# A long convolution beside local attention on one core: one manual order for the projections and the kernel generation, and a convolution in channel halves

## The chip, the core and the metric

The kernel runs on one core of a Trainium2 chip. A core has five engines with their own instruction streams: TensorE (PE in the profile, with its weight loads shown as PEld), VectorE (DVE), ScalarE (ACT), GpSimd (POOL) and SyncE (SP). Data moves between DRAM and the on-chip memory through 16 DMA engines; a transfer is started by an instruction on SP, ACT or POOL. Matmul results land in PSUM, a small memory that ACT and DVE read.

The metric is device time of one execution in microseconds (us). Lower is better. The runs of one kernel mostly agree within about 1%. Each run is marked fast or slow by its time and by the granted TensorE clock (the share of full speed at which the chip let TensorE run, 1.00 being full speed).

## The reference, cut to what matters

Two independent heads are computed and their outputs are put side by side.

```python
# head A: a state-space convolution over L = 2048 steps, D = 1024 channels, N = 128 states
P = exp(dt*A * l)                       # complex, for every step l
K = einsum("dn,dnl,dn->dl", C, P, dt*B).real          # one filter of 2048 taps per channel
y = irfft(rfft(pad(u)) * rfft(pad(K)))[:L] + u * Dskip

# head B: dilated local attention, 32 heads of 32, window 8, dilation 2
q, k, v = split(x @ wqkv)               # x is 2048 x 1024, wqkv 1024 x 3072
o = softmax(q . k[pos - 2*w], w = 0..7) @ v[pos - 2*w]
out_b = o @ wo
```

All inputs and outputs are bf16. Both kernels do the convolution as a two-step FFT with constant matrices: "step 1" multiplies u and K by a 128-wide matrix and stores the results Zu and Zk in DRAM in another order; the "middle" loads them back, transforms them further, multiplies, transforms half the way back and stores Zv (called Vd in the kernel before); "last" reads that and makes the output. Each Z array is 8.4 MB.

## The kernel before

It has three stages: (1) the projections beside the generation of K, with V after Q and K; (2) what is left of K, with step 1 of u; (3) the rest of the convolution beside attention. The parts that matter here are these (cuts are marked with "...").

```python
# V: 4096 matmuls of 128 columns
for half in range(2):
    for kt in range(KT):
        for h in range(4):
            nc.tensor.matmul(pv[32 * h:32 * h + 32, b, half * 4:half * 4 + 4, :], lhsT=xT[:, kt, t0:t0 + 32], rhs=wv[half][:, kt, :, h, :],
                             start=(kt == 0), stop=(kt == KT - 1), tile_position=(0, 32 * h))
...
# K generation: evacuation of a chunk
nc.scalar.copy(out=kraw[:, :, q0:q0 + 32].rearrange("p r (b q) -> p b q r", b=2), in_=pkv)
...
# attention: softmax without a division, by Exp and Ln in turn
nc.scalar.activation(out=pe[:], in_=S[:, :, 0:320], func=ACT.Exp, scale=scale)
...
nc.scalar.activation(out=ln[:], in_=O[:, 1, :], func=ACT.Ln)
nc.scalar.activation(out=ln[:], in_=ln[:], func=ACT.Exp, scale=-1.0)
...
# middle of the convolution: everything out of PSUM by ACT
s3 = sb.tile([128, 3, 512], BF, name="s3", bufs=4)
nc.scalar.copy(out=s3[:], in_=p3[:])
...
nc.vector.tensor_tensor(out=t12[:], in0=s3[:, 0:1, :].to_broadcast([128, 2, 512]), in1=s3[:, 1:3, :], op=ALU.mult)
...
nc.scalar.copy(out=vs[:, h * 512:(h + 1) * 512], in_=pv[:])
...
nc.scalar.dma_start(out=Vd[ri, k], in_=vs[ri * 64:(ri + 1) * 64, :])
...
# the order of the stages
_interleave([ga, gb], [1, 2], stop_on=1)                       # K generation, projections
_interleave([conv_pre(tc, S, A_u[0], "Zu", side="right"), ga], [2, 1], stop_on=0)
...
_interleave([ga, gb], [1, 1])                                  # convolution, attention
```

The softmax here doesn't subtract the row's maximum and nothing guards it: scores larger than these inputs give would overflow.

Of the kernel before, what the change touches and what calls it, by code (L numbers as in the profile page):

```python
# [18 lines left out]
def to_chunks(t):  # L19
    return t.rearrange("p (c g q) -> p g c q", c=4, g=4)  # L20


def natural(t):
    return t.rearrange("p (g c q) -> p g c q", c=4, g=4)


def kgen_params(tc, pp, tmp, A_re,A_im,B_re,B_im,C_re,C_im,log_dt):
    nc=tc.nc; V=nc.vector
    raw={}
    for nm,ap in (("Are",A_re),("Aim",A_im),("Bre",B_re),("Bim",B_im),("Cre",C_re),("Cim",C_im)):  # L30
        t=tmp.tile([128,1024],BF,name="r"+nm)
        nc.sync.dma_start_transpose(out=t[:],in_=ap)
        raw[nm]=t
    ldt=tmp.tile([128,1024],BF,name="ldt")
    nc.sync.dma_start(out=ldt[:],in_=log_dt.unsqueeze(0).to_broadcast([128,1024]))
    dt=tmp.tile([128,1024],BF,name="dt")
    nc.scalar.activation(out=dt[:],in_=ldt[:],func=ACT.Exp)
    a=pp.tile([128,1024],F32,name="p_a"); xs=pp.tile([128,1024],F32,name="p_xs")
    lnW=tmp.tile([128,1024],F32,name="lnW"); Wm=pp.tile([128,1024],BF,name="p_Wm"); phs=pp.tile([128,1024],F32,name="p_phs")
    V.tensor_tensor(out=to_chunks(a[:]),in0=natural(dt[:]),in1=natural(raw["Are"][:]),op=ALU.mult)  # L40
    v=tmp.tile([128,1024],F32,name="v"); ti=tmp.tile([128,1024],I32,name="ti")
    V.tensor_tensor(out=to_chunks(v[:]),in0=natural(dt[:]),in1=natural(raw["Aim"][:]),op=ALU.mult)
    cst=float(65536/TWO_PI)
    V.tensor_scalar(out=ti[:],in0=v[:],scalar1=cst,scalar2=None,op0=ALU.mult)
    V.scalar_tensor_tensor(out=xs[:],in0=v[:],scalar=cst,in1=ti[:],op0=ALU.mult,op1=ALU.subtract)
    lo=ti[:].bitcast(I16).rearrange("p (n two) -> p n two",two=2)[:,:,0]
    V.tensor_tensor(out=xs[:],in0=xs[:],in1=lo,op=ALU.add)
    wre=tmp.tile([128,1024],F32,name="wre"); wim=tmp.tile([128,1024],F32,name="wim"); t1=tmp.tile([128,1024],F32,name="t1"); t2=tmp.tile([128,1024],F32,name="t2")
    V.tensor_tensor(out=wre[:],in0=raw["Cre"][:],in1=raw["Bre"][:],op=ALU.mult)
    V.tensor_tensor(out=t1[:],in0=raw["Cim"][:],in1=raw["Bim"][:],op=ALU.mult)  # L50
    V.tensor_tensor(out=wre[:],in0=wre[:],in1=t1[:],op=ALU.subtract)
    V.tensor_tensor(out=wre[:],in0=wre[:],in1=dt[:],op=ALU.mult)
    V.tensor_tensor(out=wim[:],in0=raw["Cre"][:],in1=raw["Bim"][:],op=ALU.mult)
    V.tensor_tensor(out=t1[:],in0=raw["Cim"][:],in1=raw["Bre"][:],op=ALU.mult)
    V.tensor_tensor(out=wim[:],in0=wim[:],in1=t1[:],op=ALU.add)
    V.tensor_tensor(out=wim[:],in0=wim[:],in1=dt[:],op=ALU.mult)
    V.tensor_tensor(out=t1[:],in0=wre[:],in1=wre[:],op=ALU.mult)
    V.tensor_tensor(out=t2[:],in0=wim[:],in1=wim[:],op=ALU.mult)
    V.tensor_tensor(out=t1[:],in0=t1[:],in1=t2[:],op=ALU.add)
    V.tensor_scalar(out=t1[:],in0=t1[:],scalar1=1e-36,scalar2=None,op0=ALU.add)  # L60
    nc.scalar.activation(out=lnW[:],in_=t1[:],func=ACT.Ln)
    nc.scalar.activation(out=to_chunks(Wm[:]),in_=natural(lnW[:]),func=ACT.Exp,scale=0.5)
    ax=tmp.tile([128,1024],F32,name="ax"); ay=tmp.tile([128,1024],F32,name="ay")
    nc.scalar.activation(out=ax[:],in_=wre[:],func=ACT.Abs)
    nc.scalar.activation(out=ay[:],in_=wim[:],func=ACT.Abs)
    V.tensor_tensor(out=t1[:],in0=ax[:],in1=ay[:],op=ALU.max)
    V.tensor_tensor(out=t2[:],in0=ax[:],in1=ay[:],op=ALU.min)
    V.tensor_scalar(out=t1[:],in0=t1[:],scalar1=1e-30,scalar2=None,op0=ALU.add)
    V.reciprocal(out=t1[:],in_=t1[:])
    V.tensor_tensor(out=t2[:],in0=t2[:],in1=t1[:],op=ALU.mult)  # L70
    at=tmp.tile([128,1024],F32,name="at")
    nc.scalar.activation(out=at[:],in_=t2[:],func=ACT.Arctan)
    V.tensor_tensor(out=t1[:],in0=ay[:],in1=ax[:],op=ALU.is_gt)
    V.tensor_scalar(out=t2[:],in0=at[:],scalar1=-2.0,scalar2=float(np.pi/2),op0=ALU.mult,op1=ALU.add)
    V.tensor_tensor(out=t2[:],in0=t2[:],in1=t1[:],op=ALU.mult)
    V.tensor_tensor(out=at[:],in0=at[:],in1=t2[:],op=ALU.add)
    V.tensor_single_scalar(out=t1[:],in_=wre[:],scalar=0.0,op=ALU.is_lt)
    V.tensor_scalar(out=t2[:],in0=at[:],scalar1=-2.0,scalar2=float(np.pi),op0=ALU.mult,op1=ALU.add)
    V.tensor_tensor(out=t2[:],in0=t2[:],in1=t1[:],op=ALU.mult)
    V.tensor_tensor(out=at[:],in0=at[:],in1=t2[:],op=ALU.add)  # L80
    V.tensor_scalar(out=t1[:],in0=wim[:],scalar1=0.0,scalar2=-2.0*cst,op0=ALU.is_lt,op1=ALU.mult)
    V.tensor_scalar(out=t1[:],in0=t1[:],scalar1=cst,scalar2=None,op0=ALU.add)
    V.tensor_tensor(out=to_chunks(phs[:]),in0=natural(at[:]),in1=natural(t1[:]),op=ALU.mult)
    return a,xs,Wm,phs
# [15 lines left out]
def kgen(ctx, tc, A_re, A_im, B_re, B_im, C_re, C_im, log_dt, Dskip, Kd, pre=None):  # L100


    nc = tc.nc; V = nc.vector
    NCH = 4; CH = 256; Q = 64; DH = CH // 4
    pp = ctx.enter_context(tc.tile_pool(name="k_par", side="left", bufs=1))
    with tc.tile_pool(name="k_tmp", side="left", bufs=1) as tmp:
        a, xs, Wm, phs = kgen_params(tc, pp, tmp, A_re, A_im, B_re, B_im, C_re, C_im, log_dt)
        if pre is not None:
            yield from pre
    yield  # L110
    kr = ctx.enter_context(tc.tile_pool(name="k_raw", side="left", bufs=1))
    kraw = kr.tile([128, NR, 256], BF, name="kraw")
    shs, odds = shift_consts()
    shd = nc.inline_tensor(np.ascontiguousarray(shs.transpose(1, 0, 2)), name="c_sh")
    odd_d = nc.inline_tensor(odds, name="c_odd")
    shsb = kr.tile([128, 2, 128], BF, name="shsb"); odd = kr.tile([128, 2], F32, name="odd")
    nc.sync.dma_start(out=shsb[:], in_=shd.ap())
    nc.sync.dma_start(out=odd[:], in_=odd_d.ap())
    dsk = kr.tile([128, 256], BF, name="dsk")
    V.memset(dsk[:], 0.0)  # L120
    for g in range(4):
        nc.sync.dma_start(out=dsk[32 * g:32 * g + 1, :], in_=Dskip.rearrange("(o g q) -> g o q", o=1, g=4)[g])
    low16 = lambda t: t.bitcast(I16).rearrange("p j (dh dl two) -> p j dh dl two", dl=4, two=2)[:, :, :, :, 0]
    with ExitStack() as c1:
        op = c1.enter_context(tc.tile_pool(name="k_op", side="left", bufs=1))
        ph = c1.enter_context(tc.tile_pool(name="k_ph", side="left", bufs=2))
        ps = c1.enter_context(tc.tile_pool(name="k_ps", side="left", bufs=1, space=PSUM))

        E4 = pp.tile([128, 12, 1024], BF, name="E4")
        for i in range(4):  # L130
            nc.scalar.activation(out=E4[:, i, :], in_=a[:], func=ACT.Exp, scale=float(64 * i))
        for j in range(8):
            nc.scalar.activation(out=E4[:, 4 + j, :], in_=a[:], func=ACT.Exp, scale=float(8 * j))
        blk = lambda t: t.rearrange("p (dh dl) -> p dh dl", dl=4)
        for c in range(NCH):
            cs = slice(c * CH, (c + 1) * CH)
            xc = xs[:, cs]; ac = a[:, cs]; pc = phs[:, cs]; E4c = E4[:, :, cs]
            OL = op.tile([128, 2, DH, 32, 4], BF, name="OL")
            OR = op.tile([128, 2, DH, NR, 4], BF, name="OR")
            TL = op.tile([128, 2, DH, 17, 4], BF, name="TL")  # L140
            ER = op.tile([128, DH, NR, 4], BF, name="ER")
            for j, r in enumerate(RS):
                nc.scalar.activation(out=ER[:, :, j, :], in_=blk(ac), func=ACT.Exp, scale=float(r))
            yield
            for k, n in ((0, 5), (5, 4), (9, 4), (13, 4)):
                PH = ph.tile([128, 2, 5, CH], I32, name="PH")
# [3 lines left out]
                for ri in range(2):  # L150
                    nc.scalar.activation(out=TL[:, ri, :, k:k + n, :].rearrange("p dh j dl -> p j dh dl"), in_=low16(PH[:, ri, 0:n, :]), func=ACT.Sin, scale=SINSC)
# [307 lines left out]
def conv_gen(ctx, tc, S, Kd_in, outa):  # L459
# [3 lines left out]
    with ExitStack() as c2:  # L463
# [39 lines left out]
        for t in range(32 + 2):  # L503
            if t < 32:
                stage_a(t)
# [117 lines left out]
```

## Time and profile before

| | before |
|---|---|
| median of 2 runs | 906.24 us (904.7 to 907.78) |
| span of the profiled run | 907.0 us, mean granted TensorE clock 0.786 |
| busy, share of the span | PE 56%, ACT 62%, DVE 32% |
| DMA | 118.65 MB in 83,431 packets |

No engine is the limit over the whole span, so the profile has to be read by stage. The windows view of the kernel before gives, for each stretch of time, its length, each engine's busy time with its instruction count, the granted TensorE clock, the busy share of the 16 DMA engines, and GB/s:

```profile
core 0: us, PE busy (x) PEld busy (x) DVE busy (x) ACT busy (x) POOL busy (x), PEclk, DMA share, GB/s
0.00:182.00 182.00, 123.69 (x1077) 57.28 (x1088) 117.68 (x177) 117.06 (x140) 0.20 (x4) 0.95 0.44 116
182.00:300.00 118.00, 68.92 (x4127) 63.31 (x4127) 17.83 (x48) 31.92 (x46) 0.00 (x0) 0.93 0.12 40
300.00:450.00 150.00, 43.80 (x1515) 22.73 (x1519) 75.18 (x115) 89.84 (x91) 0.00 (x0) 0.56 0.41 116
450.00:545.00 95.00, 38.16 (x1115) 18.13 (x1129) 8.09 (x14) 54.52 (x61) 0.00 (x0) 0.59 0.75 220
545.00:835.00 290.00, 197.64 (x3955) 88.77 (x3985) 73.12 (x113) 244.83 (x269) 84.45 (x160) 0.81 0.51 148
```

From 182 to 300 us the core does V alone, with ACT busy 32 and DVE 18 of 118 us; from 300 to 450 it finishes K with TensorE at half clock; from 545 to 835 ACT is busy for 245 of 290 us. Two pieces of the chain of waits (start, duration, what) show what V's stretch and the end are made of; the rows between and around are left out:

```profile
239.51 1.97 PE ps L298 x128
241.48 2.03 issue
243.51 1.97 PE ps L298 x128
245.48 1.48 issue
...
870.05 20.35 DMA v<-Vd
```

About two fifths of V's time is not matmul but "issue", time in which the engine waited for nothing that the profile shows (47.4 us beside 69.4 of matmul, first row of the next view). At the end, TensorE waits 20 us for the last step's input. The groups view (line, engine, operation, shapes, count; busy us and mean ns; then idle time before them with its causes) shows V's matmuls and where ACT's time goes:

```profile
L298 PE MATMUL ps<-w,xT 128*32 128x128 bf16 x4096 | 69.4, 230 | 52.7 <-issue 47.4
L486 ACT CAST s<-p 128x1536 bf16<-128x1536 f32 x64 | 91.7, 1433 | 27.6 <-PE p L484 14.8 <-DVE pm L363 12.2 <-PE pv L498 0.6
L382 ACT ACT_TABLE_LOAD x32 | 41.1, 1283 | 10.6 <-issue 10.2
L383 ACT ACT_TABLE_LOAD x31 | 39.8, 1283 | 0.5
L185 ACT CAST kraw<-pk 128x672 bf16<-128x672 f32 x8 | 25.3, 3163 | 42.7 <-PE pk L182 42.7
```

The 63 table loads of attention, from Exp to Ln and back, cost 81 us of ACT.

### The profile page before, as it was taken

How to read it: one execution, taken by the hardware profiler on the slowest of the kernel's cores; microseconds unless marked ns; L12 is line 12 of the kernel's file. 1: busy time of each engine (PE TensorE's matmuls, PEld its weight loads, DVE VectorE, ACT ScalarE, POOL GpSimd, SP SyncE). 2: the span in 40 equal slices, each digit the busy share in tenths (PEclk: the TensorE clock that was granted, in tenths of full speed). 3: DMA queues.
4: the chain of work that ended last, by engine and by line, in shares of the span. 5: the costliest groups of instructions: out<-in, count | busy, mean ns of one | idle time of the engine just before them, and what ended most of it. 6: DMA issues, size and time to landing. Idle time of an engine off the chain costs nothing.

```text
span 907.0 us, 26183 instructions
## 1 busy us (share of the span) xinstructions
PE 506.7 (56%) x11984; PEld 263.9 (29%) x12046; DVE 292.6 (32%) x467; ACT 561.0 (62%) x628; POOL 84.6 (9%) x164
## 2 busy tenths in 40 slices
PE   0395997865555445111205464866785668754823
PEld 0142444365545211111102221332332323322301
DVE  5967841980000071487301110223222332221000
ACT  3558783781111386791308685799979997897323
POOL 0000000000000000000000002533243233300000
PEclk9997998979899666555556568977798779885977
DMA  8922323310111376600597566644584335516484
GB/s 168 197 74 92 124 74 96 102 37 35 37 51 39 124 200 177 181 2 1 125 280 253 186 160 221 201 119 117 170 248 148 104 111 153 165 33 151 107 222 148
DMA packets 83431, 118.65 MB, mean 131 GB/s; under 512 B 29941, under 2 KB 59001, under 8 KB 79737
## 3 DMA queue, kind: packets, MB, share of 16 engines
q1 hardware_dynamic: 56440, 48.80, 20.3%
q10 hardware_dynamic: 19200, 46.15, 16.6%
q0 software_dynamic: 7680, 22.03, 8.4%
q8 instruction: 94, 1.54, 0.7%
q14 instruction: 17, 0.13, 0.0%
HBM read 60.85 MB, written 50.33 MB: 123 GB/s over the span
## 4 chain that ended last, share of the span: by engine, by line
ACT 31%; PE 29%; issue 18%; DMA 7%; DVE 6%; SPq 5%; ACTq 3%; another core or an unknown queue 0%; POOL 0%; DVEq 0%
PE ps L279 11%; PE ps L298 8%; ACT s L486 6%; ACT zsb L427 4%; PE S L390 4%; ACT L383 3%; SPq L259 2%; ACT L382 2%; DMA v<-Vd 2%; ACT kraw L185 2%; ACT ln L382 2%; ACT ln L383 2%; ACT pe L361 2%; PE pz L426 2%; SPq L215 2%
## 5 line engine op out<-in xcount | busy, mean ns | idle before, releaser
L279 PE MATMUL ps<-xT,w 128*128 128x512 bf16 x501 | 117.7, 396 | 48.0 <-DMA w<-in_B_wqkv_dram 38.1
L266 ACT CAST sg<-ps 128x1024 bf16<-128x1024 f32 x48 | 48.4, 1009 | 121.1 <-PE ps L298 85.0
L486 ACT CAST s<-p 128x1536 bf16<-128x1536 f32 x64 | 91.7, 1433 | 27.6 <-PE p L484 14.8
L298 PE MATMUL ps<-w,xT 128*32 128x128 bf16 x4096 | 69.4, 230 | 52.7 <-issue 47.4
L279 PEld LDWEIGHTS <-w 128*128 128x128 bf16 x512 | 51.7, 102 | 112.8 <-DMA w<-in_B_wqkv_dram 38.1
L298 PEld LDWEIGHTS <-xT 128*32 128x32 bf16 x4096 | 63.4, 103 | 58.9 <-issue 54.0
L495 DVE TENSOR_TENSOR t<-s 128x1024 bf16<-128x1024 bf16 x64 | 44.3, 692 | 111.3 <-ACT s L486 109.7
L390 PE MATMUL S<-wosb,oT 128*128 128x512 bf16 x247 | 68.4, 409 | 19.8 <-ACT osb L392 9.6
L426 PE MATMUL pz<-ssb,l1sb 128*128 128x512 bf16 x111 | 50.1, 540 | 43.3 <-ACT zsb L427 20.8
L427 ACT CAST zsb<-pz 128x1024 bf16<-128x1024 f32 x64 | 62.7, 1020 | 18.0 <-PE pz L426 10.6
L470 POOL DMA_DIRECT2D m<-c_m x32 | 18.4, 574 | 586.8 <-DMA out_dram<-osb 561.5
L384 DVE TENSOR_TENSOR oT<-O,ln 128x512 bf16<-128x512 f32 x32 | 22.1, 692 | 154.0 <-ACT ln L383 153.9
L182 PE MATMUL pk<-OR,OL 128*32 128x21 bf16 x2048 | 21.7, 185 | 79.3 <-DVE OL L172 33.1
L167 DVE TENSOR_TENSOR OL<-E 128x2048 bf16<-128x2048 bf16 x16 | 18.8, 1215 | 137.5 <-PE pk L182 137.5
L358 PE MATMUL S<-qs,ks 32*32 32x40 bf16 (+2 forms) x2304 | 35.2, 185 | 39.8 <-DMA ks<-KT 26.5
L482 PE MATMUL p<-zu,m 128*128 128x512 bf16 x64 | 29.0, 454 | 50.1 <-ACT s L486 46.5
L185 ACT CAST kraw<-pk 128x672 bf16<-128x672 f32 x8 | 25.3, 3163 | 42.7 <-PE pk L182 42.7
L358 PEld LDWEIGHTS <-ks 32*32 32x32 bf16 x2304 | 24.6, 96 | 91.9 <-issue 63.3
L382 ACT ACT_TABLE_LOAD x32 | 41.1, 1283 | 10.6 <-issue 10.2
L159 ACT ACTIVATE OR<-PH 128x1024 bf16<-128x1024 int16 (+1 forms) x40 | 43.1, 1107 | 5.9 <-DVE PH L157 3.9
L473 POOL DMA_DIRECT2D zu<-Zu x64 | 33.4, 522 | 119.8 <-PE p L482 119.8
L182 PEld LDWEIGHTS <-OL 128*32 128x32 bf16 x2048 | 19.5, 116 | 85.4 <-issue 51.2
(105 smaller groups left out, 822.5 us busy)
## 6 DMA issues: line engine op xcount, KB each, us to landing
Zu<-zsb ACTq DMA_DIRECT2D x16, 512.0 KB, 5.8
Zk<-zsb ACTq DMA_DIRECT2D x16, 512.0 KB, 6.6
zu<-Zu POOLq DMA_DIRECT2D x64, 128.0 KB, 2.7
zk<-Zk POOLq DMA_DIRECT2D x64, 128.0 KB, 2.8
Vd<-vs ACTq DMA_DIRECT2D x64, 128.0 KB, 2.4
v<-Vd SPq DMA_DIRECT2D x8, 1024.0 KB, 14.6
w<-in_B_wqkv_dram SPq DMA_DIRECT2D x12, 512.0 KB, 5.7
m<-c_m POOLq DMA_DIRECT2D x32, 160.0 KB, 2.9
```

The source lines that it names most:

```text
L185: nc.scalar.copy(out=kraw[:, :, q0:q0 + 32].rearrange("p r (b q) -> p b q r", b=2), in_=pkv)
L266: nc.scalar.copy(out=out, in_=in_)
L279: nc.tensor.matmul(ps[:, h, :], lhsT=w[:, kt, t, c * P:(c + 1) * P], rhs=xT[:, kt, t0:t0 + 512], start=(kt == 0), stop=(kt == KT - 1))
L298: nc.tensor.matmul(pv[32 * h:32 * h + 32, b, half * 4:half * 4 + 4, :], lhsT=xT[:, kt, t0:t0 + 32], rhs=wv[half][:, kt, :, h, :], start=(k ...
L358: nc.tensor.matmul(S[hs, u, o:o + n], lhsT=ks[hs, ct, kb:kb + 32], rhs=qs[hs, ct, u * RU + qa:u * RU + qa + n], start=True, stop=True, til ...
L382: nc.scalar.activation(out=ln[:], in_=O[:, 1, :], func=ACT.Ln)
L383: nc.scalar.activation(out=ln[:], in_=ln[:], func=ACT.Exp, scale=-1.0)
L390: nc.tensor.matmul(po[:, h, :], lhsT=oT[:, ct, q0 + tt * P:q0 + (tt + 1) * P], rhs=wosb[:, ct, h * 512:(h + 1) * 512], start=(ct == 0), st ...
L426: nc.tensor.matmul(pz[:, h, :], lhsT=l1sb[:, mt, :], rhs=ssb[:, rq * 4 + rr, h * 512:(h + 1) * 512], start=True, stop=True)
L427: nc.scalar.copy(out=zsb[:, rr, :], in_=pz[:].rearrange("p a b -> p (a b)"))
L486: nc.scalar.copy(out=s3[:], in_=p3[:])
L495: nc.vector.tensor_tensor(out=t12[:], in0=s3[:, 0:1, :].to_broadcast([128, 2, 512]), in1=s3[:, 1:3, :], op=ALU.mult)
```

## The change

The intent is to make each stage use all engines at once and to unload ACT:

- The projections and the whole of K generation are put in one hand-written order on PE, ACT and DVE, so that K is complete when V is. V is done with 2048 matmuls of 256 columns in place of 4096 of 128. K's evacuation is reordered.
- The convolution runs in two halves of 512 channels. The middle handles two frequencies (k1) per tile, using 64-wide parts of the array; its product reads PSUM directly; copies go to ACT or DVE, whichever a running sum says is less loaded.
- Attention runs in units of 256 queries. One table load picks a set with exp and ln for all of it.
- All stores go through SP's queue. The middle's loads stay on POOL's queue. K is spread to its full form on chip, written to DRAM (Kd) and read back in another layout, half by half, inside step 1.

The diff is a rewrite of most of the file; this is its core (cuts marked with "...").

```diff
-                        nc.tensor.matmul(pv[32 * h:32 * h + 32, b, half * 4:half * 4 + 4, :], lhsT=xT[:, kt, t0:t0 + 32], rhs=wv[half][:, kt, :, h, :],
+                    nc.tensor.matmul(ps[32 * h:32 * h + 32, b * 256:b * 256 + 256].rearrange("p (c d) -> p c d", d=32), lhsT=self.xT[:, kt, t0:t0 + 32], rhs=self.wv[:, kt, :, h, :],
...
-                nc.scalar.copy(out=kraw[:, :, q0:q0 + 32].rearrange("p r (b q) -> p b q r", b=2), in_=pkv)
+                nc.scalar.copy(out=self.kraw[:, :, q0:q0 + 16], in_=pkv.rearrange("p q r -> p r q"))
...
+        def send(m0):
+            for g in range(4):
+                nc.sync.dma_start(out=Kd[:, 8 * m0:8 * m0 + 32, g * 128:(g + 1) * 128], in_=K[32 * g:32 * g + 32, m0:m0 + 4].rearrange("i m j q -> i (m j) q"))
+            for m in range(m0, m0 + 4):
+                nc.sync.dma_start(out=ssb[16 * m:16 * m + 16].rearrange("i (s j) d -> i s (j d)", s=2), in_=Kd[:, 8 * m:8 * m + 8, :].rearrange("(i s) j d -> i s (j d)", s=2))
...
+    with tc.manual_schedule(engines={E.PE, E.Activation, E.DVE}):
...
+        nc.scalar.add_instruction(mybir.InstLoadActFuncSet(act_func_set_id=LN_EXP, name=nc.get_next_instruction_name(), engine=E.Activation))
...
-                    nc.scalar.dma_start(out=Zv[2 * mt + b][:, r0:r0 + 4, :], in_=zsb[b * 64:(b + 1) * 64, :, :])
+                    nc.sync.dma_start(out=Z[:, n2:n2 + 4, :], in_=zs[64 * b:64 * b + 64])
...
-                s3 = sb.tile([128, 3, 512], BF, name="s3", bufs=4)
-                nc.scalar.copy(out=s3[:], in_=p3[:])
+            kf = mid.tile([128, 2, 512], BF, name="kf")
+            self.bal.copy(kf[:], F[0][:], 1024)
+            pr = mid.tile([128, 2, 2, 512], BF, name="pr")
+            for x in range(2):
+                V.tensor_tensor(out=pr[:, x], in0=F[1][:], in1=kf[:, x:x + 1, :].to_broadcast([128, 2, 512]), op=ALU.mult)
...
+            vs = mid.tile([128, 2, 512], BF, name="vs")
+            self.bal.copy(vs[:], v[:], 1024)
+            for ri in range(2):
+                nc.sync.dma_start(out=self.Z["v"][hf][4 * p + ri:4 * p + 4:2].rearrange("ab n d -> n ab d"), in_=vs[64 * ri:64 * ri + 64])
...
+    cp = ctx.enter_context(tc.tile_pool(name="cp", side="right", bufs=3, space=PSUM))
...
+    def conv():
+        u = cv.load_u(0)
+        for hf in range(2):
+            big = cv.big.tile([128, 16, 512], BF, name="big")
+            K = kt.tile([128, 8, 8, 128], BF, name="K")
+            Kd = dram.tile([32, 64, 512], BF, name=f"Kd{hf}")
+            kg.spread(hf, K, Kd, big)
+            yield from cv.step1(hf, "u", u)
+            if hf == 0:
+                u = cv.load_u(1)
+            yield from cv.step1(hf, "k", big)
+        for hf in range(2):
+            yield from cv.middle(hf)
+        for hf in range(2):
+            yield from cv.last(hf)
+    drive(conv(), 64 + 36 + 16, at.gen(), 80)
```

## The prediction

> # Prediction
>
> **What bounds the kernel before.** By the windows view:
> - 0 to 182 us (Q and K projections): TensorE busy 124 us; the first matmul starts at 38.1 us (timeline). 128x512 matmuls run at 10.74 us per 49 (chain), 0.22 us each.
> - 182 to 300 us (V): 4096 matmuls: per 128, the chain shows 1.97 us and 1.5 to 2.0 us of "issue", so 28 ns each. K generation stands still (ACT busy 32 us).
> - 300 to 450 us: the rest of K generation plus the FFT step of u, at a granted clock of 0.53 to 0.57 (ACT busy 90 us, DVE 75 us).
> - 545 to 835 us: the conv's middle with attention, ACT-bound: 245 of 290 us busy, 65 us of it 51 table loads of 1.283 us (Exp to Ln and back). The end has a 20.4 us wait for the last step's input.
>
> **What changes.**
> 1. Stage 1 (QKV beside all of K generation, one manual order). My sums from trace durations:
>  - TensorE 512x0.22=112 us; V now 2048 matmuls of 256 columns, 4096 before: at the old 28 ns about 58; K matmuls 2048 at about 20 ns, 41. Sum about 213 us, starting near 23 us, because 14 transposes at 1.42 us stand before the first matmul, not 22.
>  - ACT: 72 sines of 1.11 (80), exponentials about 45, parameters 10, evacuations 51, table loads about 18, K evacuations about 10 (8x3.16 before). Sum about 215 us.
>  - DVE about 190 us (Wm multiply and half of phase scaling gone).
>  So about 265 us with dependencies and the tail of V and K matmuls. Before, K was ready only at 445.
> 2. Stage 2 (conv and attention). Table loads go from 63 to about none: -81 us of ACT. The Trainium skill, "ScalarE: Activation LUTs", "Table sets: the hidden batching unit", says natural_log_exp_and_others has both; no trace here shows it yet. The conv middle evacuates 2x1024 columns per k1 pair on either engine, where it was 2x(2x1.43+2x0.59)=8.1 us of ACT; but the product now reads PSUM, about 1.2 us each instead of 0.69. Copies go to both engines. ACT and DVE then have about 190 us each, TensorE about 217 us at full clock (small attention matmuls about 10 ns each, timeline), about 245 at a clock of 0.85. DMA about 60 MB, 220 us of 16 engines. Three near-equal limits, so about 300 us.
> 3. About 12 us of loads between the stages, and the 20 us wait at the end hidden by prefetch: tail about 10.
>
> Sum 265+12+300+10: **590 us**, range 535 to 660. Faster by over 2%: 0.97; within 2%: 0.02; slower: 0.01.
>
> **What would show it.** First matmul near 23 us; V's "issue" halves gone into Q/K slots; last K matmul near 260; no table load after stage 1; granted clock in stage 2 above 0.8; ACT and DVE each 60 to 70% busy in stage 2; no 20 us wait at the end.
>
> **What would make it wrong.** The fixed order of stage 1 making TensorE, ACT and DVE take turns (longer than 300). The compiler still placing table loads between Exp and Ln. Three PSUM buffers of two banks shared by everything: if the product holds one for 4 us, TensorE idles, its clock falls to a half, and stage 2 takes 360. SP's queue now carries all stores: a store waiting for its data holds back the next loads.

## The result, and the profile after

The kernel after takes 689.15 us (median of 2 runs, 687.97 and 690.34), where the kernel before takes 906.24. The ratio is 0.7605, with a 95% interval of 0.7526 to 0.7684. Ratios here are the mean time of one kernel's fast runs over that of the other's fast runs of the same rounds, so they are not quite the ratio of the medians quoted. It is much faster, as predicted, but 99 us slower than the 590 predicted and outside the range of 535 to 660.

The same windows view, of the kernel after. The first row is stage 1. The second is the start of stage 2, and is contained in the third. The third, fourth and fifth rows are the three phases of stage 2, which the rest of this text calls the step-1 phase (step 1 of u and K for both halves, with attention beside it), the middle and the tail:

```profile
core 0: us, PE busy (x) PEld busy (x) DVE busy (x) ACT busy (x) POOL busy (x), PEclk, DMA share, GB/s
22.50:271.00 248.50, 208.14 (x4622) 121.74 (x4622) 173.82 (x293) 181.27 (x291) 19.17 (x17) 0.95 0.34 97
271.00:330.00 59.00, 15.42 (x457) 8.50 (x457) 17.57 (x47) 11.22 (x22) 0.00 (x0) 0.56 0.96 227
271.00:487.00 216.00, 122.73 (x3102) 61.85 (x3102) 83.76 (x151) 74.45 (x149) 7.80 (x14) 0.68 0.77 199
487.00:630.50 143.50, 111.68 (x1779) 43.95 (x1782) 87.28 (x100) 80.81 (x117) 68.22 (x115) 0.86 0.90 240
630.50:688.60 58.10, 42.35 (x772) 19.86 (x771) 21.40 (x30) 20.88 (x38) 0.00 (x0) 0.90 0.64 178
```

Stage 1 does in 271 us what was done only at 445 before (with part of step 1 of u among it). All three compute engines are 70 to 84% busy in it. Then, at 271, the picture turns over: for 59 us TensorE is busy 15, and the DMA engines are busy 96% of the time.

The groups view of the kernel after, for the lines that answer to those of before:

```profile
L399 PE MATMUL psv<-wv,xT 128*32 128x256 bf16 x2048 | 62.2, 273 | 0.0
L243 ACT CAST kraw<-pk 128x336 bf16<-128x336 f32 x16 | 7.0, 440 | 20.9 <-PE pk L239 20.9
L470 ACT ACT_TABLE_LOAD x1 | 1.3, 1283 | 0.0
L659 DVE TENSOR_TENSOR pr<-cp,kf 128x1024 bf16<-128x1024 f32 x64 | 75.7, 1219 | 42.7 <-ACT kf L499 33.5 <-PE cp L653 7.2 <-ACT ln L570 1.8
L499 ACT CAST vs<-cp 128x1024 bf16<-128x1024 f32 x32 | 32.4, 1012 | 39.8 <-DMA Zv<-vs 26.3 <-PE cp L669 12.3 <-ACT kf L499 0.9
```

TensorE no longer idles before V's matmuls (5.7 us of "issue" now stand before K's matmuls, which run between them). K's evacuation fell from 25.3 to 7.0 us. The table load of L470, at 273 us, is the last of the kernel. The product takes 1.22 us from PSUM. The last row is a new wait: ACT stands 26.3 us in the middle because the tile it wants to write, vs, is still being stored.

Where the start of stage 2 goes is shown by the timeline of the kernel after (start, duration, what, count; in brackets the idle time before it and its cause). "SPq" rows are transfers that SP starts, one after the other; a row's duration is the time SP was held by starting them. Rows of other instructions between these are left out:

```profile
272.57 0.68 SPq L616 DMA_DIRECT2D big<-in_A_u_dram  x1
273.34 14.04 SPq L295 DMA_DIRECT2D Kd<-K  x5
285.62 3.84 PE L627 MATMUL cp<-big,l 128*128 128x512 bf16 x10 [12.88 <-DMA big<-in_A_u_dram]
290.06 2.54 SPq L297 DMA_DIRECT2D big<-Kd  x4
292.63 7.86 SPq L295 DMA_DIRECT2D Kd<-K  x3
300.59 1.31 SPq L530 DMA_DIRECT2D qs<-QT  x1
301.95 0.64 SPq L532 DMA_DIRECT2D ks<-KT  x1
...
308.70 0.47 PE L550 MATMUL S<-qs,ks 32*32 32x8 bf16 x36 [15.84 <-DMA ks<-KT]
309.03 8.81 SPq L533 DMA_DIRECT2D vs<-Vt  x1
317.95 12.47 SPq L632 DMA_DIRECT2D Zu<-zs  x7
```

The trip of K through DRAM (Kd) stands first in SP's queue. Its first five writes hold SP for 14 us, 2.8 us each. The reads of Kd must wait until the writes have landed. Only then come attention's first loads, so attention's first matmul runs at 308.7. The stores of step 1's results stand behind all of these, and after 18 matmuls of step 1 its three output tiles and the three PSUM buffers are full. The chain of waits of the kernel after agrees: of its five longest pieces between 275 and 320 us, four belong to K's trip ("SPq L295" is SP starting a write of K), and one is a wait that the profile calls "issue":

```profile
275.37 4.07 SPq L295
...
285.41 4.51 DMA Kd<-K
...
293.86 9.42 DMA Kd<-K
303.36 6.42 DMA big<-Kd
...
313.85 6.58 issue
```

The second half's trip repeats this at 393 us: from 385 to 425 us the DMA share is 0.97 and TensorE is busy 23 of 40 us. Between the two, from 330 to 385, the share is 0.64 and TensorE is busy 41 of 55.

Three facts stand against three terms of the prediction. First, stage 2 moves 88 MB (199 x 216 + 240 x 143.5 + 178 x 58.1, in GB/s and us) where I had said 60, and its packets take 332 us of 16 engines (0.77 x 216 + 0.90 x 143.5 + 0.64 x 58.1) where I had said 220. Second, stage 2's sums for ACT and DVE were nearly right: 176 and 192 us against "about 190 each"; but TensorE was busy 277 us (123 + 112 + 42), against 217 at full clock and 245 at a clock of 0.85. Third, the granted clock was 0.68, 0.86 and 0.90 in the three phases, 0.77 over stage 2 weighted by their lengths, where I expected above 0.8.

### The profile page after: what moved, and what is told of

Same layout as the page of the kernel before. It is cut to its first block, busy times and chain, and to the rows that moved or that the text cites. A ratio compares the mean times of both kernels' runs of the same rounds, so it can differ in the third digit from the quotient of the medians.

```text
span 688.6 us, 23065 instructions
## 1 busy us (share of the span) xinstructions
PE 484.9 (70%) x10268; PEld 247.5 (36%) x10268; DVE 376.1 (55%) x595; ACT 369.0 (54%) x608; POOL 105.4 (15%) x163
## 4 chain that ended last, share of the span: by engine, by line
PE 35%; DVE 15%; DMA 15%; ACT 14%; issue 10%; SPq 3%; POOL 0%; ACTq 0%; DVEq 0%
PE cp L579 6%; PE ps L383 6%; DMA Zv<-vs 4%; PE psv L399 4%; DMA big<-Zv 4%; PE cp L627 3%; DVE OR L195 3%; PE O L566 3%; PE S L550 2%; PE pk L239 2%; PE cp L653 2%; DVE OL L224 2%; PE cp L669 2%; DVE OL L223 2%; DMA Kd<-K 2%
## 5 line engine op out<-in xcount | busy, mean ns | idle before, releaser
L383 PE MATMUL ps<-xT,w 128*128 128x512 bf16 x512 | 129.7, 403 | 53.7 <-DMA xT<-in_B_x_dram 32.8
L659 DVE TENSOR_TENSOR pr<-cp,kf 128x1024 bf16<-128x1024 f32 x64 | 75.7, 1219 | 42.7 <-ACT kf L499 33.5
L383 PEld LDWEIGHTS <-w 128*128 128x128 bf16 x512 | 49.1, 102 | 119.1 <-issue 61.9
L550 PE MATMUL S<-qs,ks 32*32 32x40 bf16 (+2 forms) x2304 | 38.9, 185 | 60.3 <-ACT pe L553 20.9
L579 PE MATMUL cp<-wosb,oT 128*128 128x512 bf16 x256 | 62.4, 397 | 4.7 <-ACT zs L499 2.8
L643 POOL DMA_DIRECT2D zk<-Zk x64 | 38.2, 600 | 164.3 <-PE S L550 82.9
L399 PE MATMUL psv<-wv,xT 128*32 128x256 bf16 x2048 | 62.2, 273 | 0.0
L550 PEld LDWEIGHTS <-ks 32*32 32x32 bf16 x2304 | 27.5, 96 | 93.7 <-issue 72.9
L627 PE MATMUL cp<-big,l 128*128 128x512 bf16 x128 | 43.2, 450 | 18.2 <-DMA big<-in_A_u_dram 12.9
L499 ACT CAST vs<-cp 128x1024 bf16<-128x1024 f32 x32 | 32.4, 1012 | 39.8 <-DMA Zv<-vs 26.3
L502 DVE CAST zs<-cp 128x1024 bf16<-128x1024 f32 x36 | 43.0, 1218 | 17.5 <-PE cp L627 17.4
L669 PE MATMUL cp<-pr,m 64*128 64x512 bf16 x256 | 41.2, 423 | 7.7 <-ACT vs L499 5.5
L499 ACT CAST zs<-cp 128x1024 bf16<-128x1024 f32 x28 | 28.0, 1009 | 34.2 <-PE cp L627 22.1
L182 DVE TENSOR_SCALAR PA<-PH 128x1024 int32<-128x1024 int32 (+1 forms) x36 | 27.9, 775 | 27.2 <-ACT TL L186 19.4
```

The lines of the kernel that those rows point to most:

```text
L182: V.tensor_scalar(out=PA[:, 0:n, :], in0=PH[:, 0:n, :], scalar1=16384.0, scalar2=None, op0=ALU.add)
L383: nc.tensor.matmul(ps[:, h, :], lhsT=self.w[ct][:, kt, t, :], rhs=self.xT[:, kt, t0:t0 + 512], start=(kt == 0), stop=(kt == 7))
L399: nc.tensor.matmul(ps[32 * h:32 * h + 32, b * 256:b * 256 + 256].rearrange("p (c d) -> p c d", d=32), lhsT=self.xT[:, kt, t0:t0 + 32], rhs ...
L499: self.nc.scalar.copy(out=out, in_=in_)
L502: self.nc.vector.tensor_copy(out=out, in_=in_)
L550: nc.tensor.matmul(S[hs, o:o + n], lhsT=ks[hs, ct, kb:kb + 32], rhs=qs[hs, ct, qa:qa + n], start=True, stop=True, tile_position=(32 * h, 3 ...
```

## The experiments

The theory: the step-1 phase is long because K's trip and the stores share one queue with the loads that the compute needs, in bursts; the middle is long because vs has only two tiles and a store of it lands late. The rivals: (a) stage 2 is simply bound by bytes, in whatever order; (b) three PSUM buffers are too few; (c) packets of 256 bytes in K's writes are the cost; (d) TensorE's work at a low clock is the limit.

The table has the kernel after and all 16 experiments. The phases are of the profiled run, from 271 us to about 2 us after step 1's last matmul, from there to about the last matmul of the middle's forward transform, and the rest. Each batch had its own seven runs of the kernel before on the same chip (medians 905.55 to 910.39), and the kernel after was timed only in its own two runs. So its ratio is known to about 1%, and smaller differences from it are not told apart by the time alone. The medians of f1 and e11 include slow runs; the ratios do not. The expectations of e9, e11 and f3 cut the phases at other times, so their phase lengths differ from these.

Two things have to be kept in mind in reading the phases. Each comes from one profiled execution; after, e3, e4, e5, e9 and e12, whose order of step 1 is the same, give 214.5 to 216.5 us for the step-1 phase. And attention runs beside all three phases, in 64 steps of 36 score matmuls (PE L550), of which the phases hold different numbers: 40 fall in the step-1 phase of the kernel after and of e9, 38 in that of e1 and e6, 37 in e11's, 36 in e2's, 35 in f3's and 46 in e7's. So a part of what one phase gains can be work that moved to the next, and the total time decides.

Not all expectations were met. The times of e2, e4, e6, e9 and e10 fell in the range of the branch that the text draws on. Those of e1 and e11 gained more than any branch said, those of e3, e5, e8, e12 and e14 fell between the branches, e7 and f2 fell in the branch of less gain and f3 at its edge, and f1 missed all.

| run | what is different from the kernel after | right result | median us | ratio to before | phases us |
|---|---|---|---|---|---|
| after | - | yes | 689.15 | 0.7605 | 216 / 143.5 / 58 |
| e1_no_k_trip | no trip of K through DRAM | no | 640.16 | 0.7057 | 170 / 138 / 59 |
| e2_k_act_queue | K's trip on ACT's queue | yes | 667.20 | 0.7341 | 189 / 147 / 59 |
| e3_no_zk | middle loads half | no | 677.95 | 0.7459 | 215 / 125 / 65.5 |
| e4_zu_twice | middle loads 1.5 times | yes | 694.75 | 0.7642 | 216.5 / 145 / 60.5 |
| e5_two_psum | two PSUM buffers | yes | 712.22 | 0.7837 | 216 / 158 / 65 |
| e6_more_sbuf | four tiles of zu, zk, zs, vs | yes | 666.57 | 0.7326 | 205 / 131.5 / 60 |
| e7_k_pool_queue | K's trip on POOL's queue | yes | 687.57 | 0.7558 | 224 / 131.5 / 62 |
| f1_early_k | first half of K's trip in stage 1 | yes | 700.56 | 0.7651 | 227 / 140 / 60 |
| e8_k_long_rows | K written in long rows | no | 679.01 | 0.7493 | 207 / 143 / 60 |
| e9_vs_four | four tiles of vs | yes | 677.50 | 0.7494 | 216 / 128 / 59 |
| e10_no_k_more_sbuf | e1 and e6 | no | 632.59 | 0.6985 | 170.5 / 127.5 / 60 |
| f2_order_buffers | e6, new order and queues | yes | 664.96 | 0.7338 | 189 / 147.5 / 57 |
| f3_order_buffers_sp | f2 with vs stored by SP | yes | 659.95 | 0.7270 | 188 / 138 / 60 |
| e11_no_zu_store | no stores of Zu | no | 663.21 | 0.7231 | 183 / 143 / 60 |
| e12_vs_four_no_zk | e9 and e3 | no | 670.36 | 0.7385 | 214.5 / 116.5 / 66 |
| e14_half_out_projection | e10, half of the output projection | no | 623.44 | 0.6855 | 169 / 127 / 57 |

Kernels with a wrong result leave a transfer or some work out.

### e1_no_k_trip: what K's trip costs in all

```diff
-            for g in range(4):
+            for g in range(0):
...
-            for m in range(m0, m0 + 4):
+            for m in range(0):
...
-            big = cv.big.tile([128, 16, 512], BF, name="big")
+            big = cv.load_u(hf)
```

Step 1 of K reads u instead, by one load of 2 MB for each half, so the work of the engines is the same. The trip moves 8.4 MB (4.2 written, 4.2 read), the loads in its place 4.2.

> K's trip through DRAM is taken away (the step-1 input of K is loaded from u instead, so the result is wrong on purpose): no 256-byte writes, no wait for them. If the store queue of SP is what holds up the start of stage 2 (K's 16 writes take 2.8 us each to issue, and Q/K/V loads and Zu stores stand behind them), the 59 us from the last K matmul to a steady stage 2 shrink by 25 to 40 us and the time is 650 to 665. If only bytes count, 4 MB fewer at about 230 GB/s give 17 us and the packets a few more: 665 to 672. If neither matters: 685 to 692.

It took 640.16 us, 49 less. The windows view of this run shows that the gain is in the step-1 phase (170 us instead of 216) and that the middle hardly changed:

```profile
271.00:441.00 170.00, 115.61 (x3012) 59.23 (x3012) 82.00 (x147) 72.19 (x142) 7.14 (x12) 0.77 0.75 230
441.00:579.00 138.00, 111.05 (x1913) 45.09 (x1913) 88.51 (x105) 83.23 (x123) 69.10 (x116) 0.90 0.89 249
```

Attention's first matmul is at 296.8 instead of 308.7 us. Removing 4.2 MB net would be worth about 21 us at the phase's 199 GB/s (4.2 MB / 199 GB/s); the 46 us that the phase lost are more than twice that. So it is not the bytes alone. But bytes are not time: as share times length, the 16 DMA engines worked 166 us in the phase with the trip (0.77 x 216) and 128 without (0.75 x 170), 39 less. So this run alone does not exclude that the work of the DMA engines sets the length; e2 and e4 do. What remains can be the order, the shared queue, or the size of the packets. The next runs divide these.

### e2_k_act_queue: the same trip from another queue

```diff
-                nc.sync.dma_start(out=Kd[:, 8 * m0: ...
+                nc.scalar.dma_start(out=Kd[:, 8 * m0: ...
...
-                nc.sync.dma_start(out=ssb[16 * m:16 * m + 16] ...
+                nc.scalar.dma_start(out=ssb[16 * m:16 * m + 16] ...
```

> The same K writes and reads, issued on ACT's DMA queue instead of SP's; same bytes, same packets. Queue theory: the SP queue is free for Q/K/V loads and Zu stores, 655 to 672. Bandwidth theory: no change, 684 to 694 (ACT also loses up to 45 us of issue time, of which it has plenty idle in stage 2).

It took 667.20 us, 22 less, with a right result, and the step-1 phase took 189 us. The windows row of that phase:

```profile
271.00:460.30 189.30, 115.84 (x2822) 53.93 (x2822) 80.01 (x142) 68.93 (x138) 7.15 (x12) 0.75 0.86 229
```

The bytes and the packets are those of the kernel after, and the DMA engines worked nearly as long (0.86 x 189 = 163 us, against 166); only the queue differs. So the queue is worth 22 us, a little under half of e1's gain. (The phase lost 27, but four attention steps moved into the middle, which is 3 us longer.) It is not free: starting K's first five writes now holds ACT for 15.72 us and the next three for 9.53, and the copies that ACT owes to step 1 are not done before 306 us.

### e7_k_pool_queue: the same trip from POOL's queue

The edit is that of e2, with `nc.gpsimd` in place of `nc.scalar`.

> K's writes and reads issued from POOL's software queue, which is idle until the middle. The queue theory expects at least what ACT's queue gave (667), as ACT is then free too: 655 to 668, unless writing [...]takes longer than SP's 2.8 us, then 668 to 690.

It took 687.57 us, which can't be told from the kernel after. A timeline row of this run shows why. It is attention's second load, started by SP after the load of u and attention's first load, while POOL's writes of K were running:

```profile
281.99 12.00 SPq L532 DMA_DIRECT2D ks<-KT  x1
```

Starting a single load took SP 12 us. Step 1 began at 300 us instead of 286. So another queue alone is no remedy: from POOL's queue the trip of K got in the way of the load of u and of attention's loads (the step-1 phase ended at 495 us, 8 later), and the middle is shorter (131.5 us instead of 143.5) with 10 attention steps in it instead of 16. The expectation allowed for starts on POOL that take longer than SP's 2.8 us, and the time fell in the range named for that case, but not for that reason: five writes took POOL 3.99 us, 0.8 each (its spans are rough). Why POOL's transfers held up SP's and ACT's in e2 did not is not shown. So the queue is not the whole of it: what else is moving at the same time counts too.

### e8_k_long_rows: the size of the packets

```diff
-                nc.sync.dma_start(out=Kd[:, 8 * m0:8 * m0 + 32, g * 128:(g + 1) * 128], in_=K[32 * g:32 * g + 32, m0:m0 + 4].rearrange("i m j q -> i (m j) q"))
+                nc.sync.dma_start(out=Kd[:, 8 * m0:8 * m0 + 32, :].rearrange("i (g b) d -> i g (b d)", g=4)[:, g, :], in_=K[32 * g:32 * g + 32, m0:m0 + 4].rearrange("i m j q -> i (m j q)"))
```

The same bytes of K go to DRAM, in rows of 8 KB where they were pieces of 256 bytes. They land in the wrong places, so the result is wrong.

> K's writes keep their bytes, their number, their queue and all who wait for them; only the layout in DRAM is changed (result wrong on purpose) so that each partition writes 8 KB in a row, not 32 pieces of 256 bytes. If the small packets are the cost of the K trip[...]: 655 to 670. If the trip's order and chain of waits are the cost: 683 to 692.

It took 679.01 us, 10 less, which the time alone hardly tells from the kernel after (ratio 0.7493, 0.7452 to 0.7534). But the step-1 phase took 207 us, outside the 214.5 to 216.5 of the six kernels named above. The small packets cost about 10 of the 49 us, not most of them. Rival (c) is a part and not the main cause.

### f1_early_k: half of the trip in stage 1, where the DMA engines are idle

Stage 1 keeps the DMA engines only 34% busy, so I wrote the first half of K there. The core of the edit:

```diff
                 if c % 2 == 1 and h == 1:
                     todo += [lambda hf=c // 2: kg.shift(hf)]
+                    if c == 1:
+                        todo += [lambda m=m: kg.spread_a(0, m) for m in range(8)]
...
-            kg.spread(hf, K, Kd, big)
+            if hf == 0:
+                kg.fetch(0, big)
+            else:
+                K = kt.tile([128, 8, 8, 128], BF, name="K")
+                kg.spread(hf, K, Kds[hf], big)
```

To make room, V's output tile shares the buffers of the Q and K output.

> A version meant to be kept: the first half of K, ready at about 170 us, is spread and written to DRAM inside stage 1, where the DMA engines are 34% busy and SP mostly waits; at the start of stage 2 only the reads remain. If the K trip at the start of stage 2 is the cost (its removal in both halves gave 49 us), half of it and the worse half goes: 652 to 668. If stage 1's fixed order suffers by more than 10 us, or the second half's trip costs most: 672 to 690.

It took 700.56 us (one of its four runs was slow; the three fast ones were 691.3 to 701.41), so it did not help, against my expectation. The last V matmul started at 293.6 us instead of 268.4: the copies of K and the shared tiles, not told apart, cost stage 1 about 25 us. From 271 us on, the step-1 phase with that late start ends at 498 us, 11 later than in the kernel after, so about 14 of the 25 us came back. The run neither supports nor refutes the theory; it shows that in this form the fix costs stage 1 more than it gives.

### e3_no_zk and e4_zu_twice: is the middle bound by bytes?

```diff
 # e3
-            zu = mid.tile([128, 2, 512], BF, name="zu", bufs=3); zk = mid.tile([128, 2, 512], BF, name="zk", bufs=3)
+            zu = mid.tile([128, 2, 512], BF, name="zu", bufs=3); zk = zu
...
-            for t, n in ((zu, "u"), (zk, "k")):
+            for t, n in ((zu, "u"),):
 # e4
-            for t, n in ((zu, "u"), (zk, "k")):
+            for t, n in ((zu, "u"), (zk, "k"), (zd, "u")):
```

> The middle loads no zk (zu serves for both, wrong on purpose): 8 MB and 8192 packets of 1 KB fewer in the 150 us of the middle, where the DMA engines are 90% busy. Bandwidth theory: 8 MB at 239 GB/s, so 28 to 38 us less: 652 to 662. If the PSUM ring, the product's dependencies or TensorE bound the middle: 680 to 690.

> The middle loads zu twice, the second time into a tile that nobody reads: 8 MB more, nothing waits for it but its own buffer. Bandwidth theory: 28 to 38 us more, 717 to 728. PSUM or dependency theory: 688 to 698.

e3 took 677.95 us (11 less; middle 125 us instead of 143.5, but the tail 65.5 instead of 58), e4 694.75 (6 more, which is within what the kernel after is known to; middle 145). The middle loads 16.8 MB and stores 8.4; taking away a third of its bytes took away 13% of its time. So bytes were not the only limit of the middle, though with a DMA share of 0.90 they looked like it. e4's edit missed its aim in part: many of the extra loads had no one to wait for and were started in the step-1 phase already, where POOL started 67 transfers instead of 14. But this is a finding for that phase: about 53 x 128 KB, 6.9 MB, were added to it, the DMA share went from 0.77 to 0.84, and its length stayed at 216 us:

```profile
271.00:487.50 216.50, 122.42 (x3131) 61.54 (x3120) 83.55 (x151) 74.83 (x149) 39.36 (x67) 0.69 0.84 230
```

The DMA engines worked 182 us (0.84 x 216.5) where it was 166, in a phase of the same length. Bytes that fell mostly into the gaps between the bursts cost nothing here. Rival (a) falls for the step-1 phase.

### e5_two_psum: are three PSUM buffers too few?

```diff
-    cp = ctx.enter_context(tc.tile_pool(name="cp", side="right", bufs=3, space=PSUM))
+    cp = ctx.enter_context(tc.tile_pool(name="cp", side="right", bufs=2, space=PSUM))
```

The sensitivity was measured downwards, by taking one away.

> The shared ring of two-bank PSUM tiles cut from three to two. If the ring bounds stage 2 (bandwidth having fallen for the middle: 8 MB more cost 6 us, 8 MB fewer gave 11), one tile fewer costs 40 us or more: 730 to 780. If the ring is not what the matmuls wait for: 686 to 698.

It took 712.22 us, 23 more: the middle 158 us and the tail 65, while the step-1 phase stayed at 216. So the ring of PSUM buffers matters in the middle and in the tail, and not at all in the step-1 phase. That from two to three costs this much does not show what a fourth would give; rival (b) is excluded for the longest phase only.

### e6_more_sbuf and e9_vs_four: tiles that wait for their stores

```diff
 # e9: only this; e6: this, and bufs=4 for zu, zk and zs
-            vs = mid.tile([128, 2, 512], BF, name="vs")
+            vs = mid.tile([128, 2, 512], BF, name="vs", bufs=4)
```

> One more SBUF buffer each for zu, zk and the step-1 output, two more for the middle's output, whose stores take 4 to 9 us to land with only two buffers. If the latency of the DMAs behind few buffers holds the middle (145 us) and step 1 up: 660 to 678. If bytes or TensorE bound it: 684 to 692.

> Of the buffers of e6 only those of the middle's output, four in place of two. If ACT's waits for the store of the output before it (26 us in the changed kernel's trace) hold the middle up: the middle goes from 145 to about 133 us, the time to 674 to 680. If the other buffers of e6 did it: 685 to 691.

e6 took 666.57 us, 23 less, with a right result. e9, with vs alone, took 677.50, 12 less (by the times alone this is hardly told from the kernel after, but the middle of the profiled run is clear, with the same 16 attention steps in it). The windows row of e9's middle and its group of copies into vs, to be read against the rows of the kernel after above:

```profile
487.00:615.30 128.30, 105.15 (x1808) 42.74 (x1796) 87.01 (x100) 80.83 (x117) 68.63 (x116) 0.95 0.95 268
...
L499 ACT CAST vs<-cp 128x1024 bf16<-128x1024 f32 x32 | 32.4, 1012 | 22.6 <-PE cp L669 15.6 <-DMA Zv<-vs 6.4
```

The wait on the store fell from 26.3 to 6.4 us and the middle from 143.5 to 128.3. Now the DMA engines are at 0.95 there. Of the 26.3 us in the kernel after, 16.2 came between 570 and 592 us, a stretch in which SP also starts the last step's first loads (big<-Zv) and the DMA share from 555 to 595 is 1.00: the middle too has a burst. The step-1 phase did not change in e9; in e6, where zs also has four tiles, it fell to 205.

### e12_vs_four_no_zk: what binds the middle next?

The edit is that of e9 with that of e3.

> e9 (four output buffers) and e3 (no zk loads, wrong result) together. If the DMA load reached the middle only through the landing time of its output store, which four buffers hide, nothing is added: 674 to 679. If bytes bind by themselves: 664 to 669.

It took 670.36 us. The windows row of its middle:

```profile
485.50:602.00 116.50, 100.26 (x1805) 41.47 (x1806) 86.86 (x101) 80.32 (x117) 34.50 (x58) 1.00 0.83 231
```

With a third of the middle's bytes gone and four tiles, the middle takes 116.5 us, with TensorE busy for 100 of it at full clock. So with two tiles the middle waits for stores, and with four tiles the bytes bind (0.95): without Zk it is 12 us shorter. With two tiles the bytes mattered too (e3, 125 us), probably because a store lands sooner when the DMA engines are less busy; that was not tested. That TensorE is the next limit, near 116.5 us, is argued from its 100 us of work. The limits lie close together (143.5, 128 and 116.5 us), so each single fix gives little.

### e10_no_k_more_sbuf: do the two causes add up?

The edit is that of e1 with that of e6.

> The K trip taken away as in e1 and the buffers of e6 together (wrong result). If the two costs are apart, they add: 689 - 49 - 22 = 618, range 612 to 626, and what is left over the forecast of 590 is about 28 us. If they are the same wait seen twice: 632 to 642.

It took 632.59 us. The sum of the two gains would have given 617 (689 - 49 - 23). So they overlap: the phase is 170.5 us here as in e1, so the 11 us that e6 gained there are gone, while the middle keeps its gain (127.5 us). A likely reason is that both let the step-1 phase run ahead of its stores; no run tested it.

### e11_no_zu_store: are SP's stores in the way?

```diff
-                for b in range(2):
+                for b in range(2 if name == "k" else 0):
...
-            for t, n in ((zu, "u"), (zk, "k")):
+            for t, n in ((zu, "k"), (zk, "k")):
```

Step 1 of u is computed but not stored (8.4 MB less), and the middle loads Zk twice.

> Step 1 of u stores nothing (the middle reads Zk twice; wrong result): 8 MB in 4 KB packets fewer in the step-1 phase, all evacuations and matmuls kept. If the DMA engines' work bounds that phase: 8 MB at about 20 GB/s per engine are 26 us, so the phase goes from 200 to about 175 and the time to 660 to 668. If it is the K trip's chain and its place on the queue, the phase still waits for K: 678 to 690.

Two of its four runs were slow. The fast ones took 655.89 and 658.76 us, 32 less than the kernel after, and the step-1 phase took 183 us, 33 less:

```profile
271.00:454.00 183.00, 112.20 (x2983) 56.59 (x2975) 81.64 (x146) 72.87 (x142) 7.12 (x12) 0.79 0.83 198
```

By the expectation this is the side of the DMA engines' work, and 8.4 MB at 258 GB/s (199 / 0.77) would be about 33 us (an estimate). So this run alone speaks for rival (a) as much as for the theory. Two figures speak for the theory: the DMA engines worked only 14 us less (0.83 x 183 = 152), and in e4 6.9 MB more on POOL's queue, mostly in the gaps, cost nothing. So which bytes they are counts, and not only how many. Whether the place in SP's queue or the place in time matters is not told apart, here or in e2 and f3, which move transfers in both.

### f2_order_buffers and f3_order_buffers_sp: a repair

f2 has e6's four tiles, and a new order: the first Q, K and V loads of attention stand before K's trip, wo's load after it, and the stores of zs and vs are on ACT's queue. f3 is the same, but vs is stored by SP.

```diff
-                    nc.sync.dma_start(out=Z[:, n2:n2 + 4, :], in_=zs[64 * b:64 * b + 64])
+                    nc.scalar.dma_start(out=Z[:, n2:n2 + 4, :], in_=zs[64 * b:64 * b + 64])
...
+    u0 = cv.load_u(0)
+    at.nxt = at.loads(0)
+
     def conv():
-        u = cv.load_u(0)
+        u = u0
...
             kg.spread(hf, K, Kd, big)
+            if hf == 0:
+                at.load_wo()
```

> A version meant to be kept: buffers of e6; stores of step 1 and of the middle on ACT's queue; Q/K/V of the first unit loaded before the K trip, the output weights after it. K's small packets stay. If order on SP's queue is worth what e2 showed (22 us) beside the buffers (22 us): 640 to 655. If the start of stage 2 is bound by the DMA engines, which have the same work: 658 to 668.

> As f2, but the middle's output is stored from SP's queue again (f2's step-1 phase was 166 us where e6's was 188, but its middle 142 where e6's was 133, with ACT waiting on its own queue). The gains should now add: 166 + 133 and so 648 to 658. If f2's longer middle comes from elsewhere: 660 to 668.

f2 took 664.96 us, no better than e6, and in the range that its expectation gave to a start bound by the DMA engines. The phases say otherwise: the step-1 phase fell from 205 to 189, but the middle went back from 131.5 to 147.5. Stores on ACT's queue now stand between ACT's copies; that they are the reason was not tested apart, but f3, which moves those of vs back to SP, is at 138. f3 took 659.95 us (658.37 to 665.23), ratio 0.7270 (0.7233 to 0.7306), the fastest kernel with a right result, 29 us below the kernel after, but short of the 648 to 658 of gains that add. Its interval still touches that of e6, so of the 29 us the four tiles are the sure part. The timeline of f3 answers to that of the kernel after:

```profile
274.65 5.44 SPq L530 DMA_DIRECT2D qs<-QT  x1
280.13 3.40 SPq L532 DMA_DIRECT2D ks<-KT  x1
283.58 2.69 SPq L533 DMA_DIRECT2D vs<-Vt  x1
286.37 14.44 SPq L295 DMA_DIRECT2D Kd<-K  x5
...
289.91 0.41 PE L550 MATMUL S<-qs,ks 32*32 32x8 bf16 x36 [0.42 <-DMA ks<-KT]
```

Attention starts at 289.9 us instead of 308.7, at the cost of K's trip starting 13 us later. The windows row of its step-1 phase:

```profile
271.00:458.70 187.70, 119.10 (x2807) 57.06 (x2806) 81.00 (x142) 67.67 (x134) 11.35 (x18) 0.75 0.93 241
```

The phase is 188 us, with a DMA share of 0.93 where it was 0.77. The gaps between the bursts are mostly closed, with nearly the same bytes (45 MB against 43). Against e6, the phase gained 17 us and the middle gave back 6; three attention steps moved from the one to the other. In the total the order gained 7 us over e6, which the intervals don't tell from none.

### e14_half_out_projection: is TensorE what remains?

To e10 it adds:

```diff
-                    for ct in range(8):
+                    for ct in range(4, 8):
```

for the matmuls of the output projection, so 128 of 256 are gone: about 28 us of TensorE at 0.22 us each.

> e10 (no K trip, more buffers) with half of the output projection's matmuls (128 of 128x512, about 28 us of TensorE at full clock; wrong result). If TensorE bounds what is left: 605 to 613. If DMA, ACT or the chain inside attention does: 625 to 633.

It took 623.44 us, 9 less than e10 by the medians and 12 by the ratios, of 28 possible. The middle didn't change (127 us, DMA share 0.95); the tail and the step-1 phase each lost about 2. So TensorE is part of what remains, and not its only limit. Rival (d) explains a small part.

## Why the prediction was right and wrong

Right:

- *"Faster by over 2%: 0.97."* The ratio is 0.7605.
- *Stage 1, "about 265 us".* The last K matmul started at 270.4 us and V's at 268.4. TensorE was busy 208 us against 213, in part by luck: Q and K took 130 us where I had 112 and V 62 where I had 58, but K's matmuls took 25 where I had 41. ACT was busy 193 us up to 271 (forecast 215) and DVE 184 (190). The first matmul came at 27 us, not 23. The fear that a fixed order makes the engines take turns did not come true.
- *"-81 us of ACT" by the table loads.* No load stands after L470 at 273 us. The Trainium skill, "ScalarE: Activation LUTs", "Table sets: the hidden batching unit", says that one set has exp and ln both; this trace agrees, with 1 load for 8 units of attention where there were 63.
- *"about 12 us of loads between the stages".* It was 15 us (271 to 285.6, where step 1's first matmul runs).
- *The 20 us wait at the end* is gone.
- *Stage 2's sums for ACT and DVE:* ACT 176 and DVE 192 us against "about 190 us each"; the product 1.22 us against "about 1.2".

Wrong, and it is one step: *"DMA about 60 MB, 220 us of 16 engines. Three near-equal limits, so about 300 us."* With the tail of 10 this was a forecast of 310 us from 285.6 on; it took 403. That is 93 of the 99 us missed. It has two faults.

1. **A term was mis-sized.** Stage 2 moves 88 MB and takes 332 us of 16 engines. Three Z arrays, each 8.4 MB, are written and read, which is 50 MB; with K's trip (8.4), attention's loads (13), u (4), the outputs (8) and wo (2) this makes 86. The prediction does not list the parts of its 60; with the Z arrays at half their size the same list gives 61, so that is what I counted. With 332 us the DMA engines are the largest limit and not one of three equals. With this term alone put right, my own reckoning would have given 271 + 332, about 603 us (an estimate from the phases' DMA shares above), so this fault is worth about 13 of the 99 us and the next one most of the rest.
2. **The largest sum over a stage is its time only if that work is spread over the whole stage; otherwise it is a floor. Here it was not spread.** In the step-1 phase the DMA engines are at 0.96 from 271 to 330 us and at 0.64 from 330 to 385. Shown by experiment: without K's trip the phase is 46 us shorter (e1); the same trip from ACT's queue makes it 27 us shorter, and the whole kernel 22 (e2); 6.9 MB more, mostly in the gaps, cost nothing (e4); 8.4 MB less of SP's stores save 33 us (e11); with another order, four tiles and nearly the same bytes it is 28 us shorter (f3), of which the four tiles alone gave 11 (e6), and the middle gave 6 back. In the middle, two tiles of vs make ACT wait for stores, and that is worth 15 us (e9).

A third term was off as well: TensorE, 245 us with its clock put at 0.85, was busy 277, still less than the 332 of the DMA engines. The count of 217 at full clock was about right (217 / 0.77 = 282, an estimate); the clock was not.

Of the four dangers that I named, the last was the one: *"SP's queue now carries all stores: a store waiting for its data holds back the next loads."* The direction was right, but what held back the loads was mostly K's trip, whose writes in the first half alone held SP for 22 us (14.04 + 7.86), and I gave the danger no time in the sum. The PSUM ring, another of the four, does not bind the step-1 phase at all (e5). The expected signs "granted clock in stage 2 above 0.8" and "ACT and DVE each 60 to 70% busy" failed (0.77; ACT 176 and DVE 192 of 417.6 us, 42 and 46%). The engine time was as forecast, spread over a longer stage.

What stays open: e10, which removes both causes, still takes 632.6 us, 43 more than predicted. About 9 of these are stage 1 and the gap after it. In the middle the bytes bind (0.95). How the rest divides between bytes and TensorE is not settled; e14 gave 9 to 12 of 28 us. How K's 49 us divide is settled only roughly: about 10 for small packets (e8), about 22 for the queue (e2), and these may overlap. Why the same trip from POOL's queue gained nothing (e7) is open. In the bursts, TensorE also shows waits of up to 6.6 us that the profile calls "issue" (one at 313.85); no run tested them.

## What to carry to other kernels

When a change takes the load off the compute engines, write down every array that goes through DRAM with its size, once for the write and once for the read, before calling the DMA engines "one of three limits". Then ask in which order one queue sends them: a transfer out and back that nobody needs yet should not stand before the loads that the next matmul needs. Where a store's landing frees a tile, count the tiles: two made ACT wait here, and four gave 15 us in the middle for no more than memory.

## What the Trainium skill lacked or had wrong

- "DMA: Bandwidth & Descriptors", "Issuing engines are not separate DMA queues", says that issuing from several engines "will only save the time on the sequencer it takes to initiate the DMA, which is usually small relative to the DMA itself". Here that time was not small when the DMA engines were busy: SP was held 14.04 us by five starts (2.8 us each) in the kernel after and 12.00 us by the start of one load of ks in e7, where such a start took 0.64 us in the kernel after (at 301.95 us). Moving the same transfers to ACT's queue gave 22 us (e2), to POOL's none (e7). The page lacks that starting a transfer can take longer while the DMA engines are busy, and then holds up what stands behind it on that engine.
- "DMA: Bandwidth & Descriptors", "Why small descriptors are slow (HBM only)", reckons a 256-byte piece at 11 cycles, an overhead of 27%. What such a packet costs here is not settled. From 271 to 300 us, the kernel after sent 9,101 packets, 5,767 of them under 512 bytes, with 6.76 MB at a DMA share of 0.98, and e1 sent 9,740, only 158 of them under 512 bytes, with 9.42 MB at 1.05 (the view can report slightly more than 1). If the larger packets cost the same per byte in both, I estimate about 31 ns for a 256-byte packet on one engine, about 2.4 times as much per byte as the others. e8 does not bear this out: without these packets the engines worked only about 7 us less (0.77 x 216 against 0.77 x 207), where 16,384 packets at 31 ns, less the 4.2 MB at the others' cost, give an estimate of 18. The whole effect on the time was about 10 us (e8).
- "ScalarE: Activation LUTs", "What ACT_TABLE_LOAD costs", gives about 1283 ns for the load and about 1380 ns of drain. The load's 1283 ns is in both kernels' traces. No drain beside it is: in the kernel before, a load that started at 601.10 us was followed by its activation at 602.40, and ACT idled 0.5 us in all before the 31 loads of L383.
- I found no page that says of the DMA engines that the share of a stage can be high on average and still leave the stage waiting: here a share of 0.77 over 216 us was 0.96, 0.64, 0.97 and 0.60 in its four parts, and with most gaps closed (0.93 in f3, which has four tiles too) it took 188 us with nearly the same bytes.
